# A new stored order for the tasks of a four-layer attention and gated-FFN kernel on one core

## The chip, the core and the metric

The kernel runs on one core of a Trainium2 chip. The metric is the device time of one execution in microseconds; before the change the median of three runs is 1781.42 us (1781.21 to 1782.36).

## What is computed

Four layers run one after another on a sequence of 2048 rows of width 512: attention A, FFN B, A, B, each with a layer norm ahead and a residual add behind. Attention goes through 64 segments of 32 rows. Each segment is put behind 8 memory rows, and the memory of the next segment is the attention output of those 8 rows, so the segments form a chain.

```python
for s in range(n_seg):                       # 64 segments, 32 heads of 128
    h = concatenate([mem, xs], axis=1)       # 8 + 32 = 40 rows
    q, k, v = h @ Wq, h @ Wk, h @ Wv
    p = softmax(where(mask, q @ k.T * scale, -1e9))
    o = (p @ v) @ Wo
    mem = o[:, :M, :]                        # feeds the next segment
    outs.append(o[:, M:, :])
# B: (sigmoid(x @ w_gate) * (x @ w_up)) @ w_down, inner width 1792
```

## The kernel before, in words

**Steps.** The two attention layers run interleaved: step t holds segment t of the first attention layer and segment t - 6 of the second (`LAG` is 6), so there are 70 steps. The first six and the last six hold one layer only (40 columns), the others both (80 columns). The functions are `emit_step` for a step, `ffn` for a block of four segments, `pre1`, `ln_x` and `layernorm_T` for the norms, `v_pass`, `v_half` and `strips` for the values.

**One step on TensorE.** For each group of up to six heads: q and k (L892, 24 matmuls for three heads), scores (L906), softmax on VectorE and ScalarE (L920 to L937), transposes of the probabilities (L949), probabilities times values (L975) and Wo (L993). The results of Wo for the memory rows go into the transposed input `hT` of the next step (L1006, L1011). The others go to `oxT` by a ScalarE copy (L1018, recorded at L1232); after every fourth segment `ffn` transposes `oxT` back (L1063), normalises, and runs gate and up (L1095), tanh and product (L1100, L1102) and down (L1119).

**Values.** V of the 32 rows of a segment is computed ahead for whole blocks (L695, L732), written to a scratch in HBM and read back into `vsb` (L861). V of the memory rows can only be made within the step: `strips` (L817) runs 32 matmuls on four row strips of TensorE at once, two copies bring the result to `sst`, and eight DMAs on SP's queue (four where one layer is alone, L872) spread it into `vsb`. The matmuls of L975 wait for these.

**At the start.** Rows of x are loaded on SP's queue (L779, L794), between the parts of Wv, Wq, Wk and Wo (L591). Each block of x goes through `bn_stats`, its aggregate, an add on VectorE (L651 to L653), a power on GpSimd (L654), the scaling into `xn` (L655), four transposes on TensorE (L664), and copies into `xvf` or `hT`. The first matmuls of L695 use such copies. `load_mem0` does the same without a norm for the eight first memory rows: a load (L629), four transposes (L637), two copies on VectorE (L641).

**What sets the order.** Every piece of work above is a task of the class `Planner`: an engine (or "ScalarE or VectorE"), a duration, the keys that it reads and writes, and the buffers that it takes from pools. The text `SEQUENCE` is a compressed list that gives each of the 13,280 tasks a rank. `forward` walks through a modelled time: whenever an engine is free there, it gives it the ready task with the first rank whose buffers are free. This also settles whether a copy goes to ScalarE or VectorE, whether a start-up write goes to SP's or GpSimd's queue, and which physical buffer is used. The instructions are then emitted in the order so found. On the chip every engine takes its list in order, and semaphores hold the dependences.

**Fills.** `warm` looks for gaps of over 250 ns between TensorE tasks in the modelled time and puts matmuls of zeros on the tile `hot` ahead of the task that ends the gap (L1218): in the first 8 us, and later where TensorE has been little used. A fill of n units is n times 128 columns:

```python
n = int((gap - 120.0) * (1.2 if cold else 2.4)) // P
```

**Pacing.** The large loads of FFN weights on GpSimd's queue each wait for the TensorE task that ended last ahead of them in the modelled time, so they move with the order too.

Of the kernel before, what the change touches and what calls it, by code (L numbers as in the profile page):

```python
# [20 lines left out]
P = 128  # L21
MEM = 8
SEG = 32
L = MEM + SEG
# [29 lines left out]
;Ag)rXk7pcfB%7A@!gH@5PER9zwFwU*Txh6(FIfkX|(7J?i&Gymhh!kX3<9*It9&+^ANuZ3nQF%vjb@k;)ADNDw~7A&yK6rftjYT<(0_Cu$F5_QL}_k&+#M$g4fMAuI3%VR%9II^4edG>hLecVFKKZ  # L54
fiq<zaDy4oUFv58J8W8}M`2{oi5UUb^!f*Ro0Ll?vc4MO@r^c`&wF^g&x{e8(wi=&1jnm{X}@GBNB?B98ftnN@q;Urg_TN7gRljNIZ1xL04!;{jd2yH$?cL&EwR4Y4Tqu8pK|P3tu<gW{h$`ab{UE_
fqK5_Bs&J*b^6-QBtiB1Rm-Zu8Nlc!2f&|gEyzQ&Zou|%s7^3{5zh9KTUR}tya8Oc6!P`{0)Vq8I;Cl`Bjt~AjrB%)CqD@z82Z2w;QrC0`{pXpx_R2Wh&&#2H3QIv3WnP|a@1!GQgacw;pKW^M`R|!
Nk+QQ;DjyYF5GF7!M*<sd8cVD>2uHyj70Z$6aD8lSDtqSMB#M+!9iZef2n{|jXj7clA2G^EzqM!g-lB)@}v+s<dLTg#Kii~);*dJP_OtPjOrD`dCRS`B*?af^G#|5&z)YMf)|%^UO;YbIwUZ94H|;|
&I8kZBVH%Vr|M`z4VQLMuW2mhCo%WGrCP@C3|aBQ!Z@sF?{dn1nHiX-Hcv2SE;6gPREA8v1gxUN5fjwov7s7E=){nUleMkl)rSwf-#NWnt+iLb)vYQSg8NO|ck6a&f5J`jCYy?w$`JBYrP7VoA#kkX
>yw8_VzTSGOpj8yq?_x;;hBH;rz~q4SdF9ZBg{rG@)htW>FtF!fG!q1a8hR)S^e6}q?Lzs^}+^#ob7fH!>Fyt6Ec%(XxD2g=*h~t0x*|HYIgpYBcJ&io_?o{l)`4GU_@%j@)8o~)(WjyR`I-_DVdEX
qpsq`mM61>+(8TaM-5>9Drz=jnb)-=yYKy|4I>K@zHNw@rcCC|=f*ye&WaMflMV5|xPNyTb*H)NgH9?jw1M*`|Aqy&^a*rUk;3mH)kGJznF1RvY3@t@=2^xaH0-f1Ty6gB5>G7cN@NTPLrchUmPhHP  # L60
BPzZ2ia}YU1q5^?Zh`JV^|-uLP^j5y#P_ZT06?ozV2jLQSp96AT@omT@9`T$m-yy@g4kD5^7&#?)KvIhz5<IDDn_B}S$w_%O54$*Uf&%*f!G9A0k)w2S80jRm_OzzD}%&|JCO=Jux2;jsV1&&*ocDe
vv19OW<}n=z=BXtevuQth?wJcFw3v~A;KU0Fj8U7v;-ubd1)6$LvOp^(EF2YN4lWzA>9UsIioM@psu~u&Horxi#{K)nGF~9<5jCnBT^6l!UsB(k4o)!8A~I>f8#r%yu%<R0mYyTfZ<)Sni2UT(vn0#
tm2cI5k@+Ojklj8V{nBRX$UB+gfBzr^hrH>$u5kX5;NqVjvk?&E^!9Un709~&!yGdZ`zS12GJ~~o>$PW0_Q(~(ech%@Dd4F?a@?s&4w?B3X^B#o>$WuxPHlU8E1h;6sRCPM;Cb&M89tcFI3Fc7SaL-
@ko8IZK`J@W2GEGmX}g(7vDTBKpV{0l0Fa*zKW5nQtSNYScG9m-W4oihEpRM9oZhx$s8@o43g~=;)6hTN^z^Shvggyiw$J(S&trHsZko5QCciufS!$?n=$+iEW_#~(`j}&V4WCWgYlK!d#Qs8!?9zj
+bqOxo_kt*eZ7rE@04&B0z8Nz9i<d40QttTz6^4LDi~8yhg8P4NzvULMSQJ-$b!TRs-7IAd_l8GT;#XHgZcX$-$b)HgDh{d9p!Ey5NK#kZ(Nzsu&svhey17&ct5)NozyL<4jW>hTpOmDH`UV?uNeKn
ulL27>(f<<fI2lD7P@{ZxKK5izxo4o_!^ec%pEaQr`~plAyRxTVWrISSzr8X5TfH(1GV1AzqFJC@ZL5V(+q2z_(&=mUZDhaes!D&m_4JvmfF?Tb1D<p2^ZH$QTP$`?ht%YJSK>L&CcqNEJ<!Kr{4oz
vj+K3Emf<Ch%)`ULp{|Z!2<pl7r@(XMSkbViiH_g;!i$l%ewSb&20V3maX%pZQ9=^qZ9wc+A{sGfKnIIgZi9N`Aj$1&p0a=tUVPau*9x6O+3z+=cQwW#v2L`O$oZv0t|=^q0+3wovlZqw;CjluSfY1
7;)b2dM;AEItw!IJo9aZVFG>~c1D!+Q8oJ6gHCVjgh+q=g5RV7n;S4Z{Vb-#GBbB5;S`h<JtFjk*+%dBbL|0-RP<JoBUp$?mRdco7QSmHHji-UX7~{&TCk0xhlix|OcNZzn$a?dwXxy6toswR3nCxg
<$l)jDf(|Z9;2QA2Pa?Sr*59(v?!>Gw*!qSrriD#k;zlQ3O)3BertDQxc3{@%R7C#_YLB_AsNpEq&sbpzKmH~RYP~bk{Zd_?;Wo1EPM{r9g$C}>3;0X_dxzhSf2(<dWtt@E+CAb_+p>QbPZxM{{PS3
*en5KD&!3JofsA3^5fe+Yc=aOqR)fM<|mNjpQ}L_L`b6F5Z9!0Ny_KiYa1f=>UfHv5NT}Dt#)}&@tB}*TmVzJN!1wQ308W#%Ewt9=zute@fBG_bJI~rE8@x(8H9zT)JiPkVik)hOISJpJ`Z|aqfuxS  # L70
9MY^{ThVokOpd=UmpouWZAyJ+>Q&s<TSe0J7BeE=BIr=gLszKqR~2v6Y6>hu2k+cm^UC_1#1b|?t!P7;XyfV~lp@ZnPb$}EWnWzg)_Pm2Q2jbtP7fuO#3di=k)6Dpo<n|F!K`{GgUY<TL&xEiPlsLE
&`&N90i`ZrB`F!^X2xQ#Z*X7g10f8gpm<n@MdGTPU@}*SmWq{(s7(9g_Cv(?{N1{2oaF^jfe$o_VK4qMF^xSK*{cee3e$;(u_$eW`lc&g&EI&y4i*uW%6zw-NX1hb(pOJBbt)zq^a*_i4QZU3OsA`a
ogk8T2n3iX4#2Ol?c4h;A1AqM9wA^Jr*lL?l6X!W4a}idB0|TS{P^F0xoo=H?n}?x#S)J57?AP`%qwl>;dln_?FWE@z$Yf>Vqz`|dwyR1uaTh&cJ&l`kd!X_?-X)Uh(;|b$81Dn>eA?1v=O~yq6@bR
lvtg%>-}E)I4o%t7|qUp0K%C@$IO_3Q8c<f2sy?3NQKPEsTbru3QRD|F$a4d@f{&HJW`|O6+dZE$zQ(5B{Er!7rj;f4B;-AE4MX{;f6HfmZJze6(XM=l9u^A_U!OD95{V?ww{=>wQP72Z~s4Qm*vR?
e*y&gf*;_)**=M^LbI7dC46mRe<kfr+>_l^QZ>lm(OXgC(MLi@qI+N!-8i=oU4&L8DE2q;wf%=IK%<}jzPwj}l6xHHB!-gZcv^HoZ{V!;w_?ExVSCPsDrsA{#Sb51#5b-20&?c^99>Nt=R8W4MSi*l
MCgAULe{=wE<IiLPE}6f&Z9CBTjxxm#$_7R6;Z-ebVg&LO>WXD!Pep6L3A0rMfMW?E%7v;VO`&f|Ap|wZ??;v^Q~wr_4FD&tZm<<vV<O6&>j+yJH$*U-MCo}`YUh|$58?UEU%S|;`YMe5WJlSWE_kL
E)LRM0MQ6r<a(5C^kO>B<W_mrR)FViX&=9@G;RSwumdZ&Qt1(0oIO6ak`3nRTF(wTL^pIe!t#dYVm=<rx<3Qr+huU{k!&q2AKPMS@{}fFPJPOl#O~xT)AjxxLZv|mhvohJ9z}-?!-FGN&=ldq)4r!D
*cp!V%Xw+RfahwLc)Ig{IHF)!SEG<NE#(9Yjhv#WJHTKEisY~5+qr=eRZhP)FaoF64N_9o35pnE(v8PoEVgW0r7x!jM^tenC7jjy!)MB3AcYWC48j5cMuv^}G6mD{UWyge2qtcY@;VQVZW$|axO~Oh
vJ(=-Q@Ew*P=dF|XXgO7`vJ<K48cKaSn5!FbYSw;t|wilbDVKhl?<VuNKghUS_lENW9>r$n!HW<BYwx!DFqn}AM7hQA@+s#m*u9N`b@Ma9m(V@dcecx`>pXpHMrdvT!$c6$7K*gPb#>jO6SUnwQF@S
>&t@I)gR?aZ}gYOy@|#4pu_GanAT5qv_jCS5Bv&znUe*1UBapE&|l`w?O1MdgnZ0R>Mw-E2=S@|2~OEKN1d=5kb0C<kwu$H!>xGujj568I8SGM7M8A~PmPpMktJ_zpry#uUGFxUxwuGjCr~0sf2+7g  # L80
1QQD+ok!zeEc-N#r4j85HjD_IIP7)bE0pBeVVwgpGLUF`aXcEYnas+nct*2CTatDY-UO860yp_D;wWRpnHqVob|AJG7Eu_;>7MspwFG-#th34g)A=(1$WWqkU;dyO*fYj89O$tHXy+9?G6n&!nE-bT
uHD2FL;P#J3)5yM(sJ4mXzUH7K%MW7ut6#aKE_VEm8Zy-<yJf7`JD;Ds5Y`Z;5r^JhiwaiY`Yzu+r<wjQ5Jo3qztp-Yaeftih>wiGv?Z>PImvDU$@!v+b{k6>d0r$Nyk>FDKbk@R8n3?EwnO2Jg_HM
^&{BYQ8~-q2UvBMkkT}=lF||tq88|}HA%Z!Mt#`v=86No_G8L~#*ll=e=mHZvdY}~2W}KZX>Q6&iLKNDoZhI7TM(m#F!*Py7hpHcsLyRcn)4c;_seEgk97w&NXraXv<}|Yrx`T)jmEs3KDJqcrl)v+
a`E{XIOU{=9wyfA_Qe6Fg7PICy+z0rWItXRiR_fcrE1b+YtfpKgby_i#DiZ#q>GE6gKJTEca-j*m_AZaS4r+{5`fIsD&Eka>#T$1h%?;0L<5{vRMqk<8KPEk@Hw2d(cY(lH4`Vc4`a4Z=uhAXua01S
d}N%2@j4-Sn=puE>7zRCBiN}PtDL0phD3sq=I<r8HJ|%r%nhYL7_BikjSVR7+}$I#^phFzOtMlRr9wvktyrcN>^S>5uX~y;KOZ)07B|Qpvfzi}nE<fV`fY&4nmh5Vo=gj<YM<Et2XL=k(Gfy+aAziY
!^T6yS=iPENu&kYb=FMz$XP>`DbpK9ox{*OWEvuP-dmBN%G*ZNlp2hSa77%g8H}Q_vPe%^C_Wp@)l$iHJrqj#=?~-%OjTBz7-kBg`I(xH^>eR@G<Em|wx>|WJt-xLE^W6up^P9~Kzun|byk~JEL#qF
UT%u3pg>u~N>iFXr84s{rky2t>t)1^hbyS|duHgv<R>(*@EcY|68IFb_x<JivX6sMv3lk=G4)l-D|&A(+awSm>pxhC=g<Ailb*)61+`*VtE_9f)yaAZnZx0`&xUz9Bi)0ndpC81IL=Fj>o}=}Ch^mD
a{YD<DQ#UfTxfqfn^-c6BC>YaC?R{qp)yf?p^3FV`^;lp-G8kVmKY3DqUL^S7g8+yJY4Vqq+(;q2YardKTJIIfSm;hAPuL(^{=YS2(t@2CS#O|s>c+=cuo2pLjY8Q$x#DV6Zej6Z6+s2Jao_#6eB^N
7a5P*6g-Zs{MHJT@<NVSs+drmT7C3uX>~(ur1;DdnN#UDYL?v7!!Fre<D_&r)ysX~u$jJpBXkHfi3^CbRQiN2#eVj4*Y&1Y9&Yd62}WPCU&?}1jk)^<;Xj%lk#*xH0J&?acOayDsi(r9Pg2arChoLZ
-c0{UkOgOWe7F;kG@*`6JA3Tn`bJM{0HY}ewITRwN+$1#PQS@f-e0GvY)0$_E>?k<uwxEv0N7%EmpAT;Pguj6d{Vby55>>*K-;Iy`XUw~a}xZd?9AV_f!CW0v1lx`Y@Mez3s_!eUd;`Q1*q_s7(F>=  # L90
4|BDtOk7rIPYp}7tPpCvbDyozSV)N#SL-t8I#V*{;CN%gQSVpsRe{_W<u{-?#aIGWPKK%H>**?-Ee>E?+#s+xtjt>}|33G7$N>I7i12j!u*RF%AAMnT$i@ZE-;Dgde8ZKEW37GCDnvi=le%JSa+G{n
+&Iei>EHmn=Fsxv|3C+uBlYDwTeYMZ&|8yf!>xC<lEgQzP+}DO)!F0Rf-DyHJ&<4G8eX2f+_P;6p&iv_V7UBs;C9F-9w+M|V%Dl{fMndP&kvo}d~iFsz7en-le9_u7*050e=zT3TWENVzx4zpe*EaN
E_R$wJ-6^dPSSK@HOiCva7<DlXkg9$A4q~qoev;f>xEG5`j|;}P6atT6JKHMeOBIUD!T7j@4=|Nf2Mg|DNFxWR&Hobs33JvVoFWbB(+u~7S$IxLqhyuGE&<vvl{CyO&z1oqHfh|2xyX5WdT^mjU{tL
qaiR6CykR9^~7dzlRAX3MnyC%)N&8XzzBT>bv5sR!f20Ha(j*RX9WbB&PIxchc5h=Fmjcqzgq1c{LF1WAx56-)nRxBt(DTxU^e<pf5p<J$)x~lc3BEtc>5LooO%n>XFGs~e{wNRGFTg$-_-?oHq5=9
w4PjSRCtdm*_=uiYlvVz!YpcU&k&0W4`R>fm7lQteSFF!M_52KaD|hF4CV}>6@KAW_}6k%yr)uH5D+@!u!nR>=?c#?EH^}0gd<j=cI~S7NNJIjZ-;~~8~e*@$)xkTbtoPX8<ePoaKkwZfMKsxKmi0a
GuEMV*kIW9?cN!r2{Z}sRkM}Hp5K)F0tm@-G^~vb{o~t{NOIx4)$8Ga?v>%CZ73bbqe-h(VGLXgCktybTz0o?*E>l{R4ioO9icVr#Jc5)aU&C~A(1}LPak#aaOk$ttY*Q>Q>`CmI4~tQH4Rm@q>AcG
?R9df05%CgU-Pl14SM+nGMMPk&7`&ID>$|s48-otrEtg9kZZs)L+Zk9Nq1c>2IhbA`rKc1L|lOdv395d@BqQ!ZW)c&jT3=)jt-4AomSOAN>}-+7UgX$PQR8kPkU=(C_~M3H8RWgDI*wT6%5ZSNsgs^
@`+tryad9d!c$`q7#<gIBN`WEv|-=;q=6=-NNKI5N(Z+cjzi^+wN~=rb_XnLICCEjg{eVEW=&t+zXa@WrA38tA1)DC&=s`b`b6z{%beoMIYj(s$g%D*K;Hz;p&*5f%6hl7ZLwiUm$bqc=)TbL>Z(9z
# [12 lines left out]
h9XrTN0A=!A-jepSyo2bWt}o0$3=M#E2@z-{~61_&FEpV`j(x*J9Y#toCrEC;7}hLu1j?kZtUK<@9b!NcOnRsZA8r`?+GTQTKJ}AjsZxzgG;;oek9rbeA2G40?l0gelHiXygW9NDv9YLy8r<=l&dM;  # L111
# [1186 lines left out]
```

## Time and profile before

| what | value |
|---|---|
| runs | 1781.42, 1782.36, 1781.21 us |
| span of the profiled execution, first to last instruction | 1781.3 us |
| TensorE clock granted | 1.000 |
| TensorE busy | 1754.0 us, 39873 matmul records |
| TensorE weight loads busy | 1517.1 us, 40083 records |
| VectorE, ScalarE, GpSimd busy | 1144.1, 1167.8, 573.8 us |
| moved by DMA | 270.66 MB, mean 152 GB/s |

The profiled execution has its span as its own time; the median of the runs lies 0.1 us above it. Busy time of TensorE is the time in which at least one matmul is in flight. Matmuls overlap, so a busy TensorE is not one that takes a matmul at every chance; how closely they follow each other is read from the starts in the timeline. A timeline line gives start and length in us, the engine, the line of the kernel, the operation with its tiles, how many instructions are merged, and in brackets the idle time before it and what ended it. Where a helper records a task, the line is the helper's: L1232 is every ScalarE copy, L1234 and L1226 every VectorE copy.

### The profile page before, as it was taken

What the parts mean: (1) busy time and instruction counts of PE and PEld (TensorE: products, weight loads), DVE (VectorE), ACT (ScalarE), POOL (GpSimd) and SP (SyncE); (2) the same over time, 40 slices, a digit from 0 to 9 for tenths busy, and PEclk for the clock granted to TensorE, in tenths of its full rate; (3) what the DMA queues carried; (4) which work ended last, traced back from release to release, by engine and by line L of the source; (5) the groups of instructions that cost most, each with busy time, mean ns of one, the idle gap of its engine ahead of it and who ended that gap; (6) DMA issues with size and microseconds to landing.
All of it is one profiled execution on the core that took longest, in us unless ns stands there. A gap on an engine that the chain in (4) does not pass through costs nothing.

```text
span 1781.3 us, 91977 instructions
## 1 busy us (share of the span) xinstructions
PE 1754.0 (98%) x39873; PEld 1517.1 (85%) x40083; DVE 1144.1 (64%) x3931; ACT 1167.8 (66%) x2973; POOL 573.8 (32%) x828
## 2 busy tenths in 40 slices
PE   9999999999999999999999999999999999999998
PEld 4688888888888898989898898988888888989886
DVE  4376666776577666756666676657656665666675
ACT  6676666666666666666766666666666766667564
POOL 5314031513233242323324241333324232333332
PEclk9999999999999999999999999999999999999999
DMA  9825254635555464445546453555555454555543
GB/s 342 265 74 165 59 155 121 195 105 158 146 162 153 133 174 136 139 137 165 160 130 198 135 161 106 154 160 167 156 148 172 111 145 140 158 156 139 165 143 94
DMA packets 131943, 270.66 MB, mean 152 GB/s; under 512 B 30394, under 2 KB 65090, under 8 KB 131538
## 3 DMA queue, kind: packets, MB, share of 16 engines
q0 software_dynamic: 56240, 181.91, 34.7%
q1 hardware_dynamic: 75298, 82.86, 16.3%
q8 instruction: 314, 5.14, 1.3%
q14 instruction: 91, 0.75, 0.1%
HBM read 220.41 MB, written 25.69 MB: 138 GB/s over the span
## 4 chain that ended last, share of the span: by engine, by line
PE 91%; DVE 5%; ACT 2%; issue 1%; DMA 1%; SPq 1%; POOL 0%; ACTq 0%; DVEq 0%; POOLq 0%
PE bank L892 31%; PE bank L993 17%; PE bank L1095 11%; PE bank L695 8%; PE bank L817 7%; PE bank L975 4%; PE bank L906 4%; PE bank L1119 4%; PE bank L949 2%; DVE st L920 1%; PE bank L1218 1%; PE bank L664 1%; DVE small L925 1%; DVE small L932 1%; DVE st L927 1%
## 5 line engine op out<-in xcount | busy, mean ns | idle before, releaser
L892 PE MATMUL bank<-hT,wq_sb 128*128 128x80 bf16 (+1 forms) x8960 | 622.6, 198 | 1.3 <-issue 0.6
L892 PE MATMUL bank<-hT,wk_sb 128*128 128x80 bf16 (+1 forms) x8960 | 622.5, 198 | 0.6 <-issue 0.6
L1232 ACT CAST qku<-bank 128x480 bf16<-128x480 f32 (+3 forms) x770 | 388.3, 512 | 222.5 <-PE bank L892 142.0
L892 PEld LDWEIGHTS <-wq_sb 128*128 128x128 bf16 x8960 | 454.1, 99 | 35.0 <-issue 25.1
L892 PEld LDWEIGHTS <-wk_sb 128*128 128x128 bf16 x8960 | 450.8, 99 | 0.8 <-issue 0.7
L920 DVE TENSOR_TENSOR st<-bank,cst 40x240 f32<-40x240 f32 (+3 forms) x768 | 277.7, 367 | 200.9 <-PE bank L906 194.2
L993 PE MATMUL bank<-otsb,wo_sb 128*128 128x80 bf16 (+1 forms) x8960 | 362.8, 198 | 1.9 <-ACT otsb L1232 0.2
L993 PEld LDWEIGHTS <-wo_sb 128*128 128x128 bf16 x8960 | 336.7, 99 | 16.3 <-issue 1.9
L1087 POOL DMA_DIRECT2D wg<-in_B_w_gate_dram x217 | 164.0, 756 | 299.1 <-PE bank L1095 109.8
L1232 ACT CAST otsb<-bank 128x480 bf16<-128x480 f32 (+3 forms) x420 | 199.8, 482 | 59.6 <-PE bank L975 47.6
L1088 POOL DMA_DIRECT2D wu<-in_B_w_up_dram x217 | 163.9, 756 | 197.3 <-PE bank L1095 89.3
L1113 POOL DMA_DIRECT2D wd<-in_B_w_down_dram x217 | 153.8, 709 | 213.4 <-PE bank L906 74.5
L930 ACT ACTIVATE st<-st 80x240 f32<-80x240 f32 (+3 forms) x420 | 159.5, 381 | 39.9 <-DVE st L927 37.1
L654 POOL TENSOR_TENSOR small<-small,cst 128x1 f32<-128x1 f32 (+1 forms) x80 | 44.8, 562 | 413.7 <-DVE small L653 410.2
L1095 PE MATMUL bank<-xnT,wg 128*128 128x128 bf16 (+2 forms) x1784 | 172.0, 219 | 0.8
L1095 PE MATMUL bank<-xnT,wu 128*128 128x128 bf16 (+2 forms) x1784 | 171.2, 219 | 0.0
L906 PE MATMUL bank<-qku 128*128 128x80 bf16 (+1 forms) x2240 | 161.0, 198 | 1.5 <-ACT qku L1232 0.2
L932 DVE TENSOR_REDUCE small<-st 80x6 f32<-80x240 f32 (+3 forms) x420 | 150.6, 360 | 16.3 <-ACT st L930 14.0
L937 DVE TENSOR_TENSOR pb<-st,small 80x240 bf16<-80x240 f32 (+3 forms) x420 | 153.6, 368 | 4.2
L927 DVE TENSOR_TENSOR st<-st,small 80x240 f32<-80x240 f32 (+3 forms) x420 | 154.1, 368 | 3.1
L925 DVE TENSOR_REDUCE small<-st 80x6 f32<-80x240 f32 (+3 forms) x420 | 151.4, 362 | 4.6
L975 PE MATMUL bank<-ptsb,vsb 104*128 104x80 bf16 x2048 | 140.2, 199 | 3.0 <-DMA vsb<-sst 1.5
(102 smaller groups left out, 2345.2 us busy)
## 6 DMA issues: line engine op xcount, KB each, us to landing
wg<-in_B_w_gate_dram POOLq DMA_DIRECT2D x220, 256.0 KB, 4.3
wu<-in_B_w_up_dram POOLq DMA_DIRECT2D x220, 256.0 KB, 4.3
wd<-in_B_w_down_dram POOLq DMA_DIRECT2D x220, 256.0 KB, 4.3
vsb<-scr SPq DMA_DIRECT2D x460, 48.0 KB
vsb<-sst SPq DMA_DIRECT2D x464, 32.0 KB
scr<-vst SPq DMA_DIRECT2D x112, 96.0 KB
wv_sb<-in_A_Wv_dram SPq DMA_DIRECT2D x8, 512.0 KB
wo_sb<-in_A_Wo_dram SPq DMA_DIRECT2D x10, 384.0 KB
```

The lines of the kernel that those rows point to most:

```text
L892: nc.tensor.matmul(o_ap, lhsT=W[:, c, h * P:(h + 1) * P], rhs=mv(c), start=(c == 0), stop=(c == DC - 1))
L906: nc.tensor.matmul(s_all(SB)[:, w0 + i, :], lhsT=fview(qku[:, i, 0, 0:1], [(1, P)]), rhs=qku[:, i, 1, 0:ncol], start=True, stop=True)
L920: pl.add("DVE", dve_ns(n, True), lambda gsz=gsz, hs=hs, st=st, SB=SB, pj_=pj_, npj_=npj_, mk=mk, idx=idx: nc.vector.tensor_tensor(out=st[p ...
L925: pl.add("DVE", dve_ns(n), lambda hs=hs, st=st, mx=mx: nc.vector.tensor_reduce(out=mx[pr, hs], in_=st[pr, hs], axis=AX.X, op=ALU.max), r=s ...
L927: pl.add("DVE", dve_ns(n), lambda gsz=gsz, hs=hs, st=st, mx=mx: nc.vector.tensor_tensor(out=st[pr, hs], in0=st[pr, hs], in1=mx[pr, hs].uns ...
L932: pl.add("DVE", dve_ns(n), lambda hs=hs, st=st, sm=sm: nc.vector.tensor_reduce(out=sm[pr, hs], in_=st[pr, hs], axis=AX.X, op=ALU.add), r=s ...
L975: nc.tensor.matmul(fview(OB[:, o:o + 1], [(ncol, 2), (1, L)]), lhsT=self.vsb[halves[u // 8]][0:64 + L, j, (u % 8) * P:(u % 8 + 1) * P], rh ...
L993: nc.tensor.matmul(WB[:, c * ncol:(c + 1) * ncol], lhsT=self.wo[:, h, c * P:(c + 1) * P], rhs=otsb[:, hl, 0:ncol], start=(h == 0 and c == ...
L1087: pl.add("POOL", 760, lambda wg=wg, fs=fs: nc.gpsimd.dma_start(out=wg[:], in_=self.wgv[:, :, fs]), r=[("wo", self.H - 1)], w=[gk] + bt, la ...
L1088: pl.add("POOL", 760, lambda wu=wu, fs=fs: nc.gpsimd.dma_start(out=wu[:], in_=self.wuv[:, :, fs]), r=[("wo", self.H - 1)], w=[uk] + bt, la ...
L1095: nc.tensor.matmul(gu[:, 2 * i + k, 0:n], lhsT=W[:, c, i * P:(i + 1) * P], rhs=xnT[:, c, rw], start=(c == 0), stop=(c == DC - 1))
L1232: nc.scalar.copy(out=dst, in_=src)
```

## The change

Only the text of `SEQUENCE` is replaced: 97 lines of base-85 text become 116. Code, tasks, durations, pools and tiles are untouched; the lines of the code below it move by 19 (L1218 becomes L1237, L664 becomes L683). The core of the diff, each of its lines cut short here:

```diff
 SEQUENCE = r"""
-;Ag)rXk7pcfB%7A@!gH@5PER9zwFwU*Txh6(FIfkX|(7J?i&Gymhh!kX3<9*It9&+^AN
-fiq<zaDy4oUFv58J8W8}M`2{oi5UUb^!f*Ro0Ll?vc4MO@r^c`&wF^g&x{e8(wi=&1jn
...
+;Ag)%%3S~kfFBcs-~Pwu=?-5ulZ|Ge#+zgTOFihmZKQ^29o0x3*8<kl*&>-(b`=%b!m
+wtbMy4Pt_bkw<L!QqwC<s#qtc;n;(LaskenmtQ`qOsb_cn8>-wn85|}ltZPDu0CQltip
...
 """
```

What it does is seen by laying the two built programs beside each other. On TensorE 1425 of the 4202 tasks keep their place in the list; a task moves by 2.4 places on average, by 1 in the median and by 70 at most. The matmuls that compute are the same in number and shape; the fill matmuls of zeros go from 109 to 91 (385 units of 128 columns to 311). 56 copies move from ScalarE to VectorE: among them 21 of the block copies into `hT`, 12 of those into `xnT`, and 24 of the copies of transposed probabilities into `ptsb` on balance. Four start-up writes of values go from SP's queue to GpSimd's. Waits, buffer numbers and the places of the DMAs follow from the order.

The start of three lists, before and after (names of buffers kept where they tell the blocks apart):

```
SP before:  wv, wv, x -> xs_97, x -> xs_98, x -> xs_95, x -> xa_101, x -> xs_96, x -> hff, wv, wv, wk
SP after:   wv, wv, mem0 -> hff, x -> xs_98, cst, x -> hff, x -> xs_96, x -> xs_97, wv, wv
DVE before: bn xs_97, bn xs_98, aggr x2, add x2, bn xs_96, bn hff, xn <- xs_98, ...
DVE after:  mem0 copy -> hT, bn xs_98, bn hff, aggr, bn xs_96, add, aggr x2, bn xs_97, xn <- xs_98, ...
PE before:  fill 172, L664 of xs_98, fill 21, L664 of xs_97, fill 4, L664 of hff, L695 ...
PE after:   fill 49, L637 of mem0, fill 66, L664 of xs_98, fill 15, L664 of xs_96, fill 5, L664 of xs_97, fill 4, L664 of hff, L695 ...
```

## The prediction

> **What bounds the kernel now.** I read first the page's busy times and its chain of work that ended last.
>
> ```profile
> PE   1754.0 (98%) x39873; PEld 1517.1 (85%) x40083; DVE 1144.1 (64%) x3931; ACT 1167.8 (66%) x2973; POOL 573.8 (32%) x828
> ...
> PE 91%; DVE 5%; ACT 2%; issue 1%; DMA 1%; SPq 1%; POOL 0%; ACTq 0%; DVEq 0%; POOLq 0%
> ```
>
> TensorE is the bound, so a new order can win only what TensorE loses now. How much that is comes from the starts of its matmuls in the timeline:
>
> ```profile
> 426.83 0.53 PE L993 MATMUL bank<-otsb,wo_sb 128*128 128x80 bf16 x10
> 427.88 0.40 PE L1063 MATMUL bank<-cst,oxT 128*128 128x128 bf16 x4 [0.53 <-ACT oxT L1232]
> 428.14 0.30 PE L892 MATMUL bank<-hT,wq_sb 128*128 128x80 bf16 x4
> 428.28 0.31 PE L892 MATMUL bank<-hT,wk_sb 128*128 128x80 bf16 x4
> 428.42 0.31 PE L892 MATMUL bank<-hT,wq_sb 128*128 128x80 bf16 x4
> ```
>
> Four matmuls of 80 columns start every 0.14 us, one per 36 ns, though each lasts 0.2 us. I took for each kind of TensorE task the median time from its first matmul to that of the next task (860 ns for 24 matmuls of L892, 430 for 12 of L993, 448 for 8 of L1095, 1843 for a strip) and summed over the 4202 tasks: 1723.8 us. Task starts that exceed this sum add 41.8 us; the first task starts at 11.98 us, and 3.7 us lie after the last. 11.98 + 1723.8 + 41.8 + 3.7 = 1781.3 us, the span; the median of the runs, 1781.42, is the same within their spread. So 57.5 us in all are not matmul work, and 6.5 us of the 41.8 are the switch to row strips (about 0.09 us at each strip), which any order pays.
>
> By stretch of matmul work done, the 41.8 us lie so: 3.2 in the first 80 us of work, 8.4 from 80 to 112 (first single-layer steps), 19.8 from 112 to 1600, 10.4 in the last 124. TensorE's own waits name what is behind the largest:
>
> ```profile
> PE bank L1063 <- ACT oxT L1232: 3.5, 8, 0.5
> PE bank L975 <- DMA vsb<-sst: 1.5, 2, 1.0
> ```
>
> The first is the gap shown above: the transposes of a block stand directly behind the step's last Wo matmul and wait for the copy between (0.52 or 0.69 us each). The second is late DMA, twice.
>
> **What the Trainium skill says.** "TensorE: Matmul & The Clock Gate", section "Wait — 56ns, not 53.3ns?", gives start-to-start as columns over 2.4 GHz plus about 2.5 ns when warm, columns over 1.2 GHz when cold, never under about 25 ns. The trace agrees: 216, 56, 36 and 25 ns for 512, 128, 80 and 40 columns, and the first nine fills 427 ns apart. So fills hide no cold array after 4.6 us. "Perfetto Trace Analysis", section "Identifying the Most-Contended Engine", warns against matmul busy time as a measure; here it says 98% where 1723.8 of 1781.3 us is 96.8%. "DMA: Bandwidth & Descriptors", section "Anatomy of one DMA", puts about 2 us of fixed cost on a transfer; the two late ones here took 3.00 and 3.89 us after issue, so it is met with something on top.
>
> **The change, part by part.** Matmul work stays at 1723.8 us. What changes is the start, the gaps, and the fills.
>
> *Start.* The chain begins with fills and the first norms:
>
> ```profile
> 1.00 11.14 PE L1218 MATMUL bank<-hot 128*128 128x512 bf16 x43 [1.00 <-DVE small L564]
> 11.98 0.39 PE L664 MATMUL bank<-cst,xn 128*128 128x128 bf16 x4
> 12.20 1.30 PE L1218 MATMUL bank<-hot 128*128 128x512 bf16 x6
> 13.34 0.39 PE L664 MATMUL bank<-cst,xn 128*128 128x128 bf16 x4
> 13.56 0.38 PE L1218 MATMUL bank<-hot 128*128 128x512 bf16 x1
> 13.77 0.39 PE L664 MATMUL bank<-cst,xn 128*128 128x128 bf16 x4
> 14.29 1.90 PE L695 MATMUL bank<-wv_sb,xvf 128*128 128x512 bf16 x7
> ```
>
> VectorE's timeline shows the norms that these transposes wait for:
>
> ```profile
> 9.31 0.40 DVE L655 TENSOR_SCALAR xn<-xs,small 128x512 bf16<-128x512 bf16 x1
> ...
> 10.58 0.38 DVE L655 TENSOR_SCALAR xn<-xs,small 128x512 bf16<-128x512 bf16 x1
> ```
>
> The first `xn` is ready at 9.71 us and the second at 10.96, but TensorE is still in its fills until 11.98 and 13.34: the fills are too long by 2.3 us. After, mem0 comes third on SP's queue where an x block was, whose norm began at 6.29 us when it landed; mem0 lands then at the latest. Its transposes (0.18 us) and copy (0.17) with two hand-overs put the first `bn_stats` at about 6.9, 0.6 later, since the copy heads VectorE's list. From there to the end of the first `xn` took 3.42 us with eight operations; the same eight stand there after: 10.3. The 66 fill units behind mem0 end at 6.5 + 3.6 = 10.1, so they hide. The second and third `xn` follow by VectorE's 0.6 us of small operations, the power's 0.55 and 0.4 each: 11.45 and 12.05. L664 of the third starts at 12.1; from there to L695 took 0.95 us before (13.34 to 14.29): 13.05 against 14.29. By then 1.1 us of work is done instead of 0.7, so the gain is 1.24 + 0.4 = 1.65 us. Unknown is mem0's landing: at 5.3 us the gain is 0.6 more, and if a later one holds VectorE by 1.5 us, it is near nothing. The Wv part of the first L695 is the tenth load in the queue before and after, with four x blocks ahead of it rather than six, so it lands no later.
>
> *First qk.* A fill of 7 units ended by the copy into `hT` cost 0.52 us at 28.3; there is no fill there after, as that copy and the step's matmuls have more work between. Gain 0.5.
>
> *Work 80 to 112.* Fills 75 units in 14 places before, 80 in 13 after. A unit is 53 ns and a place 120 ns more: +0.27 - 0.12 = +0.15 us.
>
> *Work 112 to 1600.* For each hand-over I compared the TensorE work that lies between producer and consumer with the time that the chain takes by the trace. Transposes with nothing between Wo and L1063: 12 before (8 of them without a fill), 11 after: -0.5. Values to Wo (L975, copy, L993) with under 1 us between: 159 before, 122 after. Softmax, with VectorE's queue counted: under 0.2 us of slack in 42 chains before and 39 after. The other way: q/k copies under 1 us, 92 before and 151 after, but only those under 0.67 us stalled, 4 before and 3 after; norms behind L1063 under 4 us of cover, 1 before and 11 after, where the chain takes 2.74 to 3.48, so four of them can lose 0.1 to 0.4: +0.5. Here I put 0. The 56 copies that leave ScalarE cost VectorE about 17 us over the whole, spread over 637 us of its idle time; not costed, and if that cover fails it is in the softmax slack just counted.
>
> *Strips to values.* SP issues the eight DMAs of a strip in 0.6 us each, so the last needed lands late. Work between strip and L975, less 0.6 us per DMA up to the one needed and 0.65 us of copies, was under 3.5 us in 11 cases and is so in 16. Two of the 11 to 12 thin ones stalled, at 1.13 and 0.68 us, each when one issue took over 1.6 us. Moved DMAs and their queues are in this count. Bounds: -1.8 (both vanish) to +2.7 (three more at 0.9); I take 0.
>
> *The last 124 us.* Fills 81 units in 13 places before, 67 in 14 after: -0.74 + 0.12 = -0.6, most of it the two before Wo and values:
>
> ```profile
> 1757.69 0.76 PE L1218 MATMUL bank<-hot 128*128 128x512 bf16 x3
> 1758.41 1.36 PE L993 MATMUL bank<-otsb,wo_sb 128*128 128x40 bf16 x48
> 1759.62 0.27 PE L949 MATMUL bank<-cst,pb 80*128 80x80 bf16 x3
> 1759.73 0.81 PE L1218 MATMUL bank<-hot 128*128 128x512 bf16 x3
> 1760.49 0.41 PE L975 MATMUL bank<-ptsb,vsb 104*128 104x80 bf16 x3
> ```
>
> There 23 units become 10 in three places. The very end (gate and up, down, output) keeps its order but for swaps of 0.2 us tasks, so its 1.04 us wait for `hff` and 3.7 us tail stay.
>
> Sum: -1.65 - 0.5 + 0.15 + 0 + 0 - 0.6 = -2.6 us, hence 1781.4 - 2.6 = 1778.8 us. Does an earlier start last? It does where TensorE runs without waits behind it; where a DMA of the weights is the limit it is swallowed. From issue to use, weights had 8.4 us at the least, so 2 us less is borne.
>
> **Rivals.** *The start gains nothing:* the mem0 row lands late and VectorE stands behind it, or the denser start waits for Wv. For it: VectorE takes its list in order, and DMA is 88% busy in the first 14 us. Against: only two Wv parts lie ahead of that row. Then only -0.5 + 0.15 - 0.6: 1780.5. *More than forecast:* the middle gains too, by both late DMAs (1.8), half a microsecond at L1063 and another in values to Wo: 1778.8 - 2.8 = 1776.0. For it: fewer thin hand-overs; against: norms and strips have become thinner. *Slower:* thin strips decide. About one in nine of SP's 516 issues takes over 1 us, and a strip's eight have to be through before L975. A late one costs 0.9 us. From three more late ones than now the 2.6 gained are gone; seven more make 1781.4 - 2.6 + 6.3 = 1785.1. Against: of 11 thin ones 2 stalled. *The order doesn't do what it says:* the lists show it does, with fills and engines changed besides.
>
> **How the numbers follow.** Forecast 0.58 (own range 1777.0 to 1780.6), start gains nothing 0.16, more 0.19, slower 0.07. A measurement of this kernel tells 0.2%, 3.6 us, from no change: faster is under 1777.9, slower over 1785.0. Faster: 0.19 and a quarter of 0.58, 0.34. Slower 0.06. Same 0.60. The range reaches from the middle of "more" to past "start gains nothing": 1775.5 to 1782.0.
>
> **What would show it.** First L695 near 13.0 us rather than 14.29; no fill at 28; 91 fill matmuls; waits of L1063 for `oxT` about 3.5 us; two or three waits of L975 for `vsb` at most; the sum of task medians still 1723.8 us. I am wrong if the starts of L892 or L993 change from 36 ns, if L975 waits for `vsb` over 4 us, or if VectorE's waits for `mem0` move the first `xn` past 11 us.

## The result, and the profile after

| | before | after |
|---|---|---|
| median of 20 runs each | 1783.39 us (1780.72 to 1785.02) | 1786.66 us (1783.38 to 1794.73) |
| span of the profiled execution | 1781.3 us | 1786.1 us |
| mean TensorE clock of the profiled execution | 1.000 | 0.999 |

The ratio is 1.0023, interval 1.0015 to 1.0032: slower by 3.3 us, where 2.6 us faster was forecast. The three runs that the forecast started from lie 2 us under the median of twenty. Below, each kernel is compared with runs of the kernel before that were taken beside it on the same chip, so the base differs a little from one experiment to the next.

The page of after, the lines that answer to the first fence of before:

```profile
PE 1766.0 (99%) x40065; PEld 1518.3 (85%) x40065; DVE 1166.8 (65%) x3987; ACT 1155.7 (65%) x2917; POOL 576.5 (32%) x832
...
PE 90%; DMA 4%; DVE 2%; SPq 2%; ACT 1%; issue 1%; POOL 0%; POOLq 0%; ACTq 0%; DVEq 0%
```

TensorE's busy time says nothing here: it grew by 12 us although there are fewer fills. Before's trace lacks 210 matmul records against its weight loads, after's none. The chain says more. DMA went from 1% of it to 4% and SP's queue from 1% to 2%, while VectorE fell from 5% to 2%. TensorE's waits in after (us in total, times, longest) name the transfer:

```profile
PE bank L994 <- DMA vsb<-sst: 5.4, 7, 1.6
PE bank L1082 <- ACT oxT L1251: 2.5, 7, 0.4
PE bank L683 <- DVE xn L674: 1.5, 2, 1.2
...
PE bank L994 <- DMA scr<-vst: 0.7, 1, 0.7
```

L994 is the old L975, L1082 the old L1063. The wait for `oxT` shrank from 3.5 to 2.5 us; the wait for strips grew from 1.5 us in two places to 5.4 in seven.

Against the same sum of task medians, 1723.8 us, the gaps by stretch of work done (profiled executions, us):

| stretch of work | before | after | difference | forecast |
|---|---|---|---|---|
| first task starts at | 11.98 | 6.03 | -5.95 | |
| 0 to 80 | 3.19 | 6.62 | +3.43 | with the line above -2.15 |
| 80 to 112 | 8.36 | 7.26 | -1.10 | +0.15 |
| 112 to 1100 | 14.07 | 15.40 | +1.33 | 0 for 112 to 1600 |
| 1100 to 1600 | 5.75 | 13.27 | +7.52 | |
| 1600 to the end | 10.44 | 10.24 | -0.20 | -0.6 |

The start gives 2.5 us, and 7.5 us are lost in one stretch. Its largest place, in TensorE's timeline of after:

```profile
1155.56 0.59 PE L1138 MATMUL bank<-wd,hff 128*128 128x512 bf16 x2
1155.99 0.20 PE L994 MATMUL bank<-ptsb,vsb 104*128 104x80 bf16 x1
1156.98 0.27 PE L994 MATMUL bank<-ptsb,vsb 104*128 104x80 bf16 x3 [0.79 <-DMA vsb<-sst]
1158.32 0.54 PE L994 MATMUL bank<-ptsb,vsb 104*128 104x80 bf16 x8 [1.07 <-DMA vsb<-sst]
...
1160.20 1.80 PE L1012 MATMUL bank<-otsb,wo_sb 128*128 128x80 bf16 x24
1161.80 0.40 PE L968 MATMUL bank<-cst,pb 80*128 80x80 bf16 x3
```

The first matmul of L994 is followed by two holes, 1.9 us of waiting for strips. The chain of waits over this stretch (start, length, what) tells why:

```profile
1148.66 1.75 SPq L891
...
1152.35 0.59 SPq L891
...
1152.98 5.20 DMA vsb<-sst
...
1158.32 0.54 PE bank L994 x8
```

One issue of the strip took 1.75 us where 0.59 is usual, and the last DMA took 5.20 us to land. In those microseconds GpSimd issued five weight loads of 256 KB:

```profile
1150.24 0.78 POOL L1106 DMA_DIRECT2D wg<-in_B_w_gate_dram  x1 [4.61 <-PE bank L1114]
1151.25 1.60 POOL L1107 DMA_DIRECT2D wu<-in_B_w_up_dram  x2 [0.22 <-issue]
1153.75 0.75 POOL L1106 DMA_DIRECT2D wg<-in_B_w_gate_dram  x1 [0.90 <-PE bank L925]
1155.85 0.75 POOL L1106 DMA_DIRECT2D wg<-in_B_w_gate_dram  x1 [1.35 <-PE bank L925]
```

A further cost follows the hole. In the timeline the 24 Wo matmuls at 1160.20 take 1.60 us to the next task, 67 ns each where 36 is the rule. A table of the stretch (length, busy time of the five engines, granted clock, DMA share, GB/s) shows the clock at half:

```profile
1159.30:1162.70 3.40, 3.40 (x52) 3.40 (x50) 0.86 (x4) 1.62 (x5) 1.31 (x2) 0.50 0.38 104
```

3.4 us at half the clock do up to 1.7 us less work. No such window lies within the work of the profiled execution of before.

The theory after this: the new order gains at the start what was forecast, and loses more than that from thin cover between strips and values, where a strip's DMA lands late behind weight loads. Rivals: the new order is worse throughout, the moved copies above all; or the early start collides with something later.

### The profile page after: what moved, and what is told of

It reads as the page before. It is cut to its first block, busy times and chain, and to the rows that moved or that the text cites. A ratio compares the mean times of both kernels' runs of the same rounds, so it can differ in the third digit from the quotient of the medians.

```text
span 1786.1 us, 92123 instructions
## 1 busy us (share of the span) xinstructions
PE 1766.0 (99%) x40065; PEld 1518.3 (85%) x40065; DVE 1166.8 (65%) x3987; ACT 1155.7 (65%) x2917; POOL 576.5 (32%) x832
## 4 chain that ended last, share of the span: by engine, by line
PE 90%; DMA 4%; DVE 2%; SPq 2%; ACT 1%; issue 1%; POOL 0%; POOLq 0%; ACTq 0%; DVEq 0%
PE bank L911 31%; PE bank L1012 16%; PE bank L1114 10%; PE bank L714 7%; PE bank L836 7%; PE bank L1138 5%; PE bank L994 4%; PE bank L925 4%; PE bank L968 2%; DMA vsb<-sst 1%; SPq L891 1%; DMA wv_sb<-in_A_Wv_dram 1%; PE bank L683 1%; DMA wg<-in_B_w_gate_dram 1%; DVE st L939 1%
## 5 line engine op out<-in xcount | busy, mean ns | idle before, releaser
L911 PE MATMUL bank<-hT,wk_sb 128*128 128x80 bf16 (+1 forms) x8960 | 622.4, 198 | 0.5 <-issue 0.5
L911 PE MATMUL bank<-hT,wq_sb 128*128 128x80 bf16 (+1 forms) x8960 | 622.4, 198 | 0.3
L911 PEld LDWEIGHTS <-wq_sb 128*128 128x128 bf16 x8960 | 455.2, 99 | 25.7 <-issue 14.5
L911 PEld LDWEIGHTS <-wk_sb 128*128 128x128 bf16 x8960 | 450.5, 99 | 0.6 <-issue 0.6
L1114 PE MATMUL bank<-xnT,wg 128*128 128x128 bf16 (+2 forms) x1784 | 171.6, 218 | 0.6 <-DMA wg<-in_B_w_gate_dram 0.6
L1114 PE MATMUL bank<-xnT,wu 128*128 128x128 bf16 (+2 forms) x1784 | 171.2, 218 | 0.0
L994 PE MATMUL bank<-ptsb,vsb 104*128 104x80 bf16 x2048 | 139.1, 199 | 7.4 <-DMA vsb<-sst 5.4
```

The source lines that it names most:

```text
L911: nc.tensor.matmul(o_ap, lhsT=W[:, c, h * P:(h + 1) * P], rhs=mv(c), start=(c == 0), stop=(c == DC - 1))
L994: nc.tensor.matmul(fview(OB[:, o:o + 1], [(ncol, 2), (1, L)]), lhsT=self.vsb[halves[u // 8]][0:64 + L, j, (u % 8) * P:(u % 8 + 1) * P], rh ...
L1114: nc.tensor.matmul(gu[:, 2 * i + k, 0:n], lhsT=W[:, c, i * P:(i + 1) * P], rhs=xnT[:, c, rw], start=(c == 0), stop=(c == DC - 1))
```

## The experiments

**Half of the order at a time.** Two kernels with ranks joined from both lists at rank 5640, about 1,770 of the 4,202 TensorE tasks. Only the text of `SEQUENCE` differs; what the new text stands for, in words:

```diff
-rank = after                                         # all ranks
+rank = after[:5640], then the rest as in before      # first kernel
+rank = before[:5640], then the rest as in after      # second kernel
```

Expected of the first: 

> The new order for the first 1,770 TensorE tasks (to about 770 us), the old order for the rest. Theory (late strips): the new order is really about 4 us faster in its first 600 us and loses about 9 us from there to 1600 us because L975 waits for the values of strips. Then this kernel gains: about 3 to 4 us less than the kernel before, ratio 0.998. Rival (the new order is worse everywhere, or its start gain is an artefact of the one profiled execution): ratio 1.000 to 1.002.

Expected of the second: 

> The old order for the first 1,770 TensorE tasks, the new order for the rest. Theory (late strips): all of the loss and none of the gain, 6 to 8 us over the kernel before, ratio 1.0035 to 1.0045, with five or more waits of L975 for vsb in its second half. Rival (the loss is spread evenly): about half of the 3.3 us, ratio 1.001.

Measured: the new order first 1780.97 us, 0.9985 (0.9979 to 0.9992) of before's 1783.70; the new order last 1789.36, 1.0033 (1.0021 to 1.0046). So -2.7 and +5.7 us, where -3 to -4 and +6 to +8 were expected: both a little short, the signs and the split as the theory has them. Their sum, +2.9, is about the +3.3 of the whole change. The gain of the early start is still there at the end, with no sign of a collision; the loss needs only the last part. Waits in the second kernel, whose L986 is L994 of after:

```profile
PE bank L986 <- DMA vsb<-sst: 6.0, 7, 1.4
PE bank L1074 <- ACT oxT L1243: 2.8, 7, 0.5
```

The first kernel waits 0.8 us for strips. It beats both kernels.

**No strip DMAs.** A strip holds 32 rows of values: for each of two segments its 8 memory rows and 8 rows of the segment itself (only the other 24 of the segment's rows are made ahead, `XS = 24`). In both orders the 516 DMAs that carry these rows from `sst` to `vsb` are left out; the rows are zeroed once at the start instead, by a second edit that isn't shown, and the matmuls stay.

```diff
-... nr=nr: nc.sync.dma_start(
+... nr=nr: None and nc.sync.dma_start(
```

Expected in the old order: 

> The old order with the DMAs from sst to vsb (L872) left out, 516 of them; the rows of vsb that they would write are zeroed once at the start, so the values of memory rows and late rows are missing from the sums. Every other task, its place and its buffers stay. Theory (late strips): before loses about 1.8 us to these DMAs in the profiled execution, so it becomes 1.5 to 2.5 us faster than the kernel before.

Expected in the new order: 

> The new order with the same 516 DMAs left out. Theory (late strips): without them the new order shows its start gain, 3 to 4 us under the old order without them, so 5 to 6 us under the kernel before (ratio 0.997). Rival (something else in the new order is slow, queues of ScalarE and VectorE or loads of FFN weights): it stays 3 us over the old order without them, so about 1 us over the kernel before.

Measured: old order 1779.72 us, 0.9979 (0.9972 to 0.9986); new order 1777.66, 0.9966 (0.9954 to 0.9978). The sign turns: without strip DMAs the new order is 2.1 us the faster, with them 3.3 the slower. So 5.4 us of the difference hang on the strip DMAs. Moved copies and thinner norms, which stay in these kernels, are not what makes after slow. The new order came out 6 us under before, as expected; its lead over the old order is 2.1 us and not 3 to 4, because the old order won 4.0 us where 1.5 to 2.5 were expected. Strip DMAs cost the old order too, and more than the 1.5 us that its one trace shows.

**No weight loads.** Of the FFN weights only the first load into each buffer is made, so blocks compute with old weights; the strips stay. One of three lines that are edited alike:

```diff
-lambda wg=wg, fs=fs: nc.gpsimd.dma_start(out=wg[:], ...
+lambda wg=wg, fs=fs, bt=bt: bt and nc.gpsimd.dma_start(out=wg[:], ...
```

Expected in the new order: 

> The new order with the FFN weight loads on GpSimd's queue left out after the first of each buffer (3 of each kind stay, and those of the last block), so later blocks compute with the weights of the first; all other tasks keep their places, the strip DMAs too. Theory (the strips' packets queue behind the packets of weight loads on the same DMA engines): the waits of L994 for vsb<-sst fall from 5.4 us to under 1 us, and the kernel comes to 1778 to 1780 us, as without the strip DMAs. Rival (SP issues the eight DMAs too slowly, now and then over 1 us each, and the work between strip and use is too short for that alone): the waits stay above 3 us, and the time above 1783 us.

Expected in the old order: 

> The old order with the same weight loads left out. Theory (queueing behind weight loads): 1779.5 to 1781.5 us, slower than the new order without the loads by about 2 us. Rival (slow issue): 1782 to 1784 us, and not slower than the new order without the loads.

Measured: new order 1776.42 us, 0.9972 (0.996 to 0.9983) of 1781.02; old order 1778.91, 0.9988 (0.9981 to 0.9994). The new order is 2.5 us the faster, and its waits for strips are down to

```profile
PE bank L994 <- DMA vsb<-sst: 0.9, 2, 0.6
```

with all 516 strip DMAs and the thin cover in place. That is what the theory asked for: waits under 1 us, and a lead near 2 us. SP's issues are no faster there: 57 of the 516 still took over 1 us, 347 us in all. So a slow issue alone doesn't make TensorE wait, and thin cover costs little once the weight loads are gone. Which resource strips and weight loads share, the DMA engines or the memory behind them, these runs don't part.

**A larger landing time in the plan.** The planner counts a strip's DMA as landed 3.2 us after its issue. Two kernels count 4.2 in the new order and 4.7 in the joined order of the first experiment, where both layers are in step:

```diff
-... lat=3200.0, use=[sb], nb=nr * 2048)
+... lat=4200.0 if both else 3200.0, use=[sb], nb=nr * 2048)
```

Expected of 4.2 us: 

> The new order with one number of the planner changed: where both layers are in a step, a strip DMA counts as landed 4.2 us after its issue, not 3.2 us. The planner then keeps L975 later; strips with under 4 us left after issue fall from 34 to 5, under 5 us from 70 to 64, and 56 units of fill come in. Theory (too little time between issue and landing was planned): the waits for vsb<-sst fall to about 2 us, less 1 to 2 us for new planned gaps: 1782 to 1784 us. Rival (landing time isn't the cause): no faster than the new order, 1786.7 us or more.

Expected of 4.7 us: 

> The kernel of e1 (new order to about 770 us, old order after) with strip DMAs counted as landed 4.7 us after issue where both layers are in a step. Theory: e1 loses about 0.8 us to late strips, and the plan pays 25 more units of fill (1.3 us), so about as e1: 1780 to 1782 us. If late strips cost e1 more than its one profile shows, it is faster than e1, 1779 us.

Measured: 1799.35 us, 1.0100 (1.0083 to 1.0116), and 1796.71, 1.0086 (1.0072 to 1.0100). Both missed by 14 us and more. The wait for strips did fall, to 2.2 us in the first and out of the list in the second, whose waits are now led by copies:

```profile
PE bank L1066 <- ACT oxT L1235: 4.6, 11, 0.5
PE bank L996 <- ACT otsb L1235: 3.5, 7, 0.9
```

With another duration the same greedy walk over the same ranks gives another plan: from 112 to 1600 us of work the second kernel has 35.1 us of gaps where before has 19.8. These two don't separate the theories.

**The thin steps alone.** To vary the cover's effect without a new plan, strip DMAs are left out in 12 of the 58 two-layer steps, with the order untouched: once in the 12 steps after step 26 where L994 had stood 0.2 us or more for a strip in the trace of after or in that of the kernel with the new order last, once in 12 others. In these steps the rows of the strips keep old values.

```diff
-... nr=nr: nc.sync.dma_start(
+... nr=nr: t not in (29, 32, 39, 42, 44, 48, 54, 56, 58, 61, 62, 63) and nc.sync.dma_start(
```

Expected of the stalled twelve: 

> The new order with the 8 strip DMAs of 12 of the 58 two-layer steps left out, the steps in which the values' matmuls were seen to stall for vsb after step 26 (in the profile of after, or in that of the run with only the last part new); those steps use old memory-row values, so part of the computation is left out. Theory 'a few thin steps' (what the new order loses is lost where the cover between strip and values became thin): L994 waits for vsb fall from 5.4 us to about 1, most of the 5 us that separate it from an order without such stalls is gone: 4 to 6 us below the after of 1786.7, some 0.998 to 1.000 of the kernel before. Rival 'strip DMAs cost by their number' (issue, queue and bandwidth, spread over all steps): 12 of 58 steps give 12/58 of the 9 us that leaving out all 516 gave, 1.9 us, ratio near 1.001 to 1.002.

Expected of the others: 

> The control: the new order with the strip DMAs of 12 other two-layer steps left out (12, 17, 19, 23, 28, 30, 34, 36, 40, 45, 50, 52), none of which stalled; those steps use old memory-row values, so part of the computation is left out. Theory 'a few thin steps': L994 waits for vsb stay about 5 us and the time falls by under 1 us, ratio 1.0015 to 1.0025 of the kernel before. Rival 'by their number': 1.9 us as in the other run, and the same ratio in both.

Measured: the stalled twelve 1779.92 us, 0.9977 (0.9967 to 0.9988) of 1784.29; the others 1784.65, 1.0003 (0.9993 to 1.0012). By the ratios, leaving out 96 DMAs wins 8.2 us against after in the steps that stalled (0.9977 against 1.0023) and 3.6 in the others: 4.7 us, by the medians, hang on which steps they are. The wait for strips in the first:

```profile
PE bank L994 <- DMA vsb<-sst: 0.6, 2, 0.4
```

In the second it is 1.9 us in five places, with 0.9 more for `scr`. It was expected to stay near 5: a miss, though steps that had stalled in after still wait in it. Its gaps from 1100 to 1600 us of work are 7.9 us, the first's 5.5, like before. So most of the effect sits in the thin steps. The rival isn't empty: both won more than expected, and the control was to win under 1 us. The intervals of its ratio and of after's allow 0.5 us as well as 7. Three of its twelve steps had a slack under 4 us in the new order, and its profiled execution lost 1.7 us at one L911 for nothing that the profile shows, with a half-clock window right behind it. So I can't say how the 3.6 us divide. The difference between the two kernels doesn't rest on the clock: among executions with a mean clock of 1.000, six of the first have a median of 1779.7 us and seven of the second 1783.9, 4.1 apart.

## Why the prediction failed, step by step

**Start and first qk: right.** Forecast -1.65 and -0.5, together -2.15 us; the gaps to 80 us of work give -2.5, the joined kernel -2.7 for its whole first part. That the sum fits so well is in part luck, as the parts show. The transposes of the first `xn` started when the fills ended:

```profile
7.74 2.21 PE L1237 MATMUL bank<-hot 128*128 128x512 bf16 x10
9.79 0.39 PE L683 MATMUL bank<-cst,xn 128*128 128x128 bf16 x4
...
11.42 0.40 PE L683 MATMUL bank<-cst,xn 128*128 128x128 bf16 x4
...
12.38 3.63 PE L714 MATMUL bank<-wv_sb,xvf 128*128 128x512 bf16 x16
```

The first L695, now L714, came at 12.38 us, not 13.05: the third `xn` stood in its transposes at 11.42 rather than 12.1, and from there the 0.95 us taken from before held (0.96). So L714 was 1.9 us earlier than L695, not 1.24, and some of it was given back: L714 waited for Wv for 0.37 us at 27.5, where the forecast saw the loads with room. FFN weights, too, for which it counted 8.4 us at the least, kept L1114 waiting for 0.6 us in two places.

**Work 80 to 112: small, wrong sign.** Counting fill units gave +0.15 us, the trace -1.1.

**Work 112 to 1600: the step that failed.** The part *strips to values* said: "under 3.5 us in 11 cases and is so in 16 ... I take 0", with +2.7 us as its upper bound. The mechanism was right and the limit was taken from the wrong place. 3.5 us lay between the two late landings of before, 3.00 and 3.89 us; in after the decisive one took 5.20. With the same arithmetic (work between strip and L975, less 0.6 us per DMA and 0.65 us of copies) and other limits, values tasks under the limit:

| limit, us | all 420: before | after | work 112 to 1600: before | after |
|---|---|---|---|---|
| 3.5 | 11 | 17 | 2 | 8 |
| 4.0 | 35 | 49 | 20 | 34 |
| 4.5 | 48 | 70 | 28 | 48 |
| 5.0 | 61 | 96 | 37 | 70 |

The forecast's 11 and 16 (17 in this recount) were over the whole program; in the stretch for which the 0 was meant it is 2 against 8. Of the 58 two-layer steps, those with a smallest slack under 4 us go from 15 to 23. The twelve stalled ones had 6.0 us of it on average before, and 3.8 after. The new order spends slack down to the 3.2 us that the planner counts, which costs nothing in its model. At the one limit that was counted five cases were added, over the whole program; at those from 4 to 5 us, which a landing of 5.20 us exceeds, 14 to 35.

**The size.** The term was 0, and measured: 5.4 us by leaving out strips, 5.8 by leaving out weight loads (3.3 + 2.5), 4.7 by the twelve steps over their control. TensorE's waits at L994 for strips and values from `scr` account for 4.9 us in one execution (5.4 + 0.7 + 0.3 against 1.5), and the half-clock window for up to 1.7. That window was in no term. How much of the median it makes stays open: the eight of after's 20 executions with a mean clock of 1.000 have a median of 1784.6 us, 1.2 over before's, but an execution that stalls more may also be the one that loses clock.

**SP's issue times didn't change.** The rival pointed at issues over 1 us. In both traces 56 of the 516 took that long, 347 and 348 us in all. What changed is how much work stands behind a long one.

**The last 124 us: right sign, a third of the size.** Forecast -0.6, measured -0.2.

**The base.** It rested on three runs and on the span as the execution's own time. The device time of after lies 1.7 to 1.8 us above the span in each of its executions, so before's profiled execution belongs at about 1783.0, beside its median of twenty.

**The chance.** The rival *thin strips decide* had the place, the mechanism and, at 1785.1 or 1.0021 times its base, the size. It got 0.07, on "of 11 thin ones 2 stalled". That was one execution of before, and one trace shows one draw of which strips come late. The prediction's own test, "if L975 waits for `vsb` over 4 us", came true.

## What to carry to other kernels

When an order is re-searched against a model, look at what the model says is free: slack above a modelled landing time gets spent, and here 5 us were then paid for landings later than the model's number. Count hand-overs against the longest landing that any trace shows beside competing loads, not against the late ones of one run, and count at several limits, since a growth at all of them is the warning. Changing one duration didn't repair a tuned list of ranks in either of two tries; joining it with another list at one rank, as the first experiment did, kept the part that wins.

## What the runs showed of the hardware that was not expected

- A transfer of 32 KB from SBUF to SBUF took 5.20 us from issue to landing while five 256 KB loads were issued within 6 us; the two late ones of before took 3.00 and 3.89. Without the weight loads TensorE's waits for such transfers fell from 5.4 us to 0.9, though as many issues took over 1 us.
- TensorE's clock record fell to 0.5 in the midst of a warm kernel twice in the twelve traces, for 3.41 us each time: in after at 1159.32 us, and in the control of the last experiment at 126.42. In the 3.41 us just before, TensorE was busy for 1.54 and 1.49 us and stood still for the rest, in after in several holes. The next most that it stood in 3.41 us, in any trace and once the start is over, is in the new order without strip DMAs: busy 1.66 us there, and the clock stayed. (Length, busy time of PE, PEld, DVE, ACT and POOL, clock, DMA share, GB/s; the stretch before and the one at half clock for each of the two, and last the stretch that kept its clock.)

```profile
1155.91:1159.32 3.41, 1.54 (x20) 0.92 (x18) 2.69 (x12) 1.15 (x4) 0.85 (x2) 1.00 0.45 147
1159.32:1162.73 3.41, 3.41 (x52) 3.41 (x50) 0.89 (x4) 1.63 (x5) 1.29 (x2) 0.50 0.39 106
...
123.01:126.42 3.41, 1.49 (x52) 1.27 (x48) 1.94 (x7) 1.38 (x6) 0.00 (x0) 1.00 0.13 35
126.42:129.83 3.41, 3.26 (x49) 2.59 (x50) 2.37 (x10) 2.21 (x9) 0.75 (x1) 0.50 0.11 18
...
168.90:172.31 3.41, 1.66 (x35) 1.06 (x32) 1.32 (x5) 1.03 (x7) 2.20 (x5) 1.00 0.68 192
```

  So holes close together may count as a sum; two cases are a pointer and no rule. The kernel with the new order last fits it: it waited 6.0 us in all for strips, never stood over 1.5 us within 3.41 us, and shows 1.000 in all five executions.
- A mean clock under 1.000 is no proof of lost work. Of after's 20 executions 12 have one, and those with 0.998 took 1789.4 to 1794.7 us. But three of the six of the new order without weight loads have 0.999 at no longer time, and in the profiled one the record at 0.5 begins after the last matmul.
- The new order's executions scatter over 11 us, the old one's over 4. With the stalled twelve steps' strips left out, seven executions lie within 5 us; fourteen of the control, which keeps those strips, scatter over 9.
